# Softmax sums of unit 14 inverted over DRAM instead of on TensorE, and w4 tile 14 in two parts around the scores of unit 15

## The chip, the cores and the metric

The kernel runs on one core of a Trainium2 chip (trn2). The metric is the device time of one execution in microseconds; the median of three runs of the kernel before is 199.16 us (199.09 to 200.41). One further execution was profiled.

The engines are named as the profile names them: PE (TensorE, matmuls) and PEld (its weight loads), DVE (VectorE), ACT (ScalarE), POOL (GpSimd) and SP (SyncE, which here only issues DMAs). Each engine carries out its instructions in the order of the program; between engines there are semaphores. A DMA can be issued from SP, ACT or POOL.

## What is computed

A sequence of 2048 rows of 512 (bf16) is normalised and goes through two branches, A (attention) and B (two small MLPs), which are multiplied in a gate:

```python
xn = _layernorm(x)
# A: 32 heads of 16, each query sees 8 keys, at distances 0, 2, ..., 14 before it
q, k, v = split(xn @ wqkv)
attn = _softmax(where(mask, (q . kg) * scale, -1e9))   # kg, vg: gathered keys, values
s = concat_heads(attn . vg) @ wo
# B
h  = _gelu(_layernorm(xn) @ w1)
hs = shifted_quarters(h) @ w2
x1 = xn + hs
h2 = _gelu(_layernorm(x1) @ w3) @ w4
g  = _silu(x1 + h2)
return x + s * g
```

## The kernel before, in words

**Tiling.** The rows are kept as even rows (p = 0) and odd rows (p = 1), 1024 each, since the attention's distances are all even. A row tile is 128 rows; tile t = 8p + i, with i from 0 to 7. The first part (up to about 104 us) computes q, k and branch B up to the GELU of w3 (h3). The rest is a loop over **17 attention units** n = 0 to 16. Unit 0 holds the first rows of both halves, and units 1 to 8 (p = 0) and 9 to 16 (p = 1) hold 120 queries each.

**One iteration n**, in the order in which each engine gets its instructions:

- `scores(n)`, 32 small PE matmuls (L603) into PSUM `s` (4 banks); `weighted(n - 1)`, 64 PE matmuls (L650) of the previous unit's probabilities by its values into PSUM `o`. The lhs holds, beside each head's 16 values, 16 columns of the constant 2, so the softmax sums come out as rows of the same product. DVE adds the 8 columns where two key blocks meet (`mix`, L666, L667), and the function that `weighted` returns, called as `evict()`, copies the rest to SBUF on ACT (L668). Both write the tile `orw`.
- `exps(n)`, ACT (L614) from `s` to `prob`; `within(n)`, DVE (L623), cuts `prob` to the window.
- `values(n + 1)`, 4 PE matmuls (L582) into bank `b`, copied by ACT (L587).
- `w4_part(n, lo, hi)`, up to 11 PE matmuls (L529) of w4 for row tile n into bank `w`; with the last of them DVE adds the tile of x1 (L537), and the tile is put on a list of gates. `CUT` is 6. Tile 15 adds x1 on PE with an identity (L535).
- `gate_tanh` (ACT, L555) and `gate_mult` (DVE, L561) make the gate by a tanh for tiles up to 13; `gate_silu` (ACT, L547) by SiLU, whose table is loaded at L922, for tiles 14 and 15.
- from n = 6, `final(p, i)`: 4 PE matmuls (L802) by wo into bank `b`; its gate multiplies on DVE (L813, or L811 where the gate was made by SiLU with a factor 2) and adds x on POOL (L818); `store` writes two tiles (L844).

There is one bank `w`, one bank `b`, and one pair `o`. A matmul that starts a new use of a bank waits until the reader of the old use is done.

**Sums.** Units are joined in 11 runs. Runs 1 to 6 have two units each (run 6 is units 11 and 12), runs 7, 8, 9, 10 are units 13, 14, 15, 16. `moves` (L693) copies the 8 blocks of heads of `orw` to `oT`, one DMA each, on SP and POOL. The product in `oT` still has to be multiplied by the inverse of its softmax sum, and there are two ways for it:

- over DRAM, runs 0 to 7: `sums_gather` (two DMAs, L679, to `dn`), `sums_invert` (DVE reciprocal L757, then a DMA to DRAM, L759), `sums_read` (a DMA, L765, that spreads each inverse over 16 partitions and overwrites `orw`, so it also waits for the run's moves), `sums_apply` (L773, on DVE, for run 7 on POOL);
- on TensorE, runs 8, 9, 10: `sums_turn` (8 matmuls, L703), `sums_inverse` (DVE reciprocal L711 and two ACT copies L716), `sums_back` (4 matmuls, L741), `sums_mult` (DVE, L750, from PSUM). Runs 9 and 10 also go to `oT` by `rows` (8 matmuls L728, ACT copy L733) instead of moves.

**Which end which.** `final(1, i)` reads columns 128 i to 128 i + 127 of `oT`. With p = 1, run 7 is columns 544 to 663, run 8 664 to 783, run 9 784 to 903, run 10 904 to 1023. So final(1,4) needs run 7, final(1,5) runs 7 and 8, final(1,6) runs 8 and 9, final(1,7) runs 9 and 10.

**The order** is the one written in the program: at its end every instruction is made to follow the one before it on its engine. What is issued on one queue is therefore held up by a wait of anything ahead of it there. `R` is 11, `NN` is 17, `NC` is 3.

Of the kernel before, what the change touches and what calls it, by code (L numbers as in the profile page):

```python
# [15 lines left out]
def kernel(  # L16
# [22 lines left out]
    NF = (F + P - 1) // P  # L39
# [19 lines left out]
    NC = 3  # L59
# [462 lines left out]
    def w4_part(t, lo, hi, tag="w"):  # L522
        c, jj = t // TPC, t % TPC
        if lo == 0:
            banks["w4", t] = pst(tag, "w4_ps")[:, 0, :]
        pt = banks["w4", t]
        for ft in range(lo, hi):
            fs = P if ft < NF - 1 else FL
            pe.matmul(  # L529
                pt, lhsT=h3[c][:fs, ft, jj * P : (jj + 1) * P], rhs=w4_sb[:fs, ft, :],  # L530
                start=(ft == 0), stop=(ft == NF - 1 and t < NN - 2),
            )
        x_i = x_tile(c, jj)
        if hi == NF and t == NN - 2:
            pe.matmul(pt, lhsT=ident[:], rhs=x_i, start=False, stop=True)  # L535
        elif hi == NF:
            dve.tensor_tensor(out=x_i, in0=pt, in1=x_i, op=ALU.add)  # L537
            gates.append(t)
# [11 lines left out]
    def gate_tanh():  # L550
        for t in gates:
            if ("sig", t) in banks:
                continue
            sig = fin.tile([P, D], BF16, name="sig", tag="f")
            act.activation(sig, x_tile(t // TPC, t % TPC), AF.Tanh, scale=0.5)  # L555
            banks["sig", t] = sig
# [11 lines left out]
    def values(n):  # L568
        p, u = order[n]
        va = v_aug[n % NV]  # L570
        vp = pst("b", "v_ps")[:, 0, :]
        for dt in range(ND):
            first, last = dt == 0, dt == ND - 1
            if p is None:
                for s in range(2):
                    pe.matmul(
                        vp[KB * s : KB * s + KB, :], lhsT=xnT[s][:, dt, 0:KB], rhs=wv_sb[:, dt, :],
                        start=first, stop=last, tile_position=(0, KB * s),
                    )
            else:  # L580
                k0 = units[u]
                pe.matmul(vp, lhsT=xnT[p][:, dt, k0 : k0 + P], rhs=wv_sb[:, dt, :], start=first, stop=last)  # L582
        vs = vp.rearrange("p (h d) -> p h d", d=DH)
        if n == 0:
            dve.tensor_copy(out=va[:, :, 0:DH], in_=vs)  # L585
        else:
            act.activation(va[:, :, 0:DH], vs, AF.Copy)  # L587
        vas[n] = va
# [82 lines left out]
    rden = {}  # L671
    R = len(runs)

    def sums_gather(i):

        _, a, b, _, rw, parts = run_of(runs[i][0])
        dn = small.tile([P, H * rw // P], BF16, name="dn", tag="dn")
        for j in range(2):
            sp.dma_start(  # L679
                out=dn[P // 2 * j : P // 2 * (j + 1), :], in_=orw[i][DH : P : 32, ND * j : ND * (j + 1), :]  # L680
            )
        rden[i] = dn

    def moves(i, queues, part=None, heads=range(8)):

        _, a, b, _, rw, parts = run_of(runs[i][0])
        w = orw[i]
        for p, q0, c, nq in parts if part is None else [parts[part]]:
            if p not in oT:
                oT[p] = (midt if p == 0 else bigt)([P, ND, M], f"oT{p}")  # L690
            for hh in heads:
                jj, cg = divmod(hh, 4)
                queues[hh % len(queues)].dma_start(  # L693
                    out=oT[p][DH * hh : DH * (hh + 1), :, q0 : q0 + nq],
                    in_=w[32 * cg : 32 * cg + DH, ND * jj : ND * jj + ND, c : c + nq],
                )

    def sums_turn(i, tag):

        w = orw[i]  # L700
        pt = pst(tag, "dt_ps")[:, 0, 0:H].rearrange("p (g c) -> p g c", c=4)
        for g in range(2 * ND):
            pe.matmul(pt[0:QU, g, :], lhsT=w[:, g, :], rhs=ident[:, DH::32], start=True, stop=True)  # L703
        rden[i] = pt

    def sums_inverse(i, copy=lambda: None, behind=False):

        pt = rden[i]
        rb = small.tile([P, 2 * ND, 4], BF16, name="rbt", tag="rbt")
        with nc.allow_low_precision("bf16 weights"):  # L710
            dve.reciprocal(out=rb[0:QU], in_=pt[0:QU])  # L711
        if not behind:
            copy()
        rx = slot().rearrange("p (s j c d) -> p s j c d", s=ND, j=2, c=4)
        for j in range(2):
            act.activation(  # L716
                rx[0:QU, :, j], rb[0:QU, j * ND : (j + 1) * ND, :].unsqueeze(3).to_broadcast([QU, ND, 4, DH]), AF.Copy
            )
        if behind:
            copy()  # L720
        rden[i] = rx
# [46 lines left out]
    def sums_apply(i, eng=dve):  # L768
        _, a, b, _, rw, parts = run_of(runs[i][0])
        rr = rden.pop(i).rearrange("p (s q) -> p s q", s=ND)  # L770
        for p, q0, c, nq in parts:
            o = oT[p][:, :, q0 : q0 + nq]
            eng.tensor_tensor(out=o, in0=o, in1=rr[:, :, c : c + nq], op=ALU.mult)  # L773
# [69 lines left out]
    def store(q, p, i, n=2, cs=slice(0, D)):  # L843
        q.dma_start(  # L844
            out=ov[p, i * P : (i + n) * P, cs].rearrange("(i q) d -> q i d", q=P),
            in_=xo[p, i & ~1][:, i % 2 : i % 2 + n, cs],
        )
# [4 lines left out]
        load_xo(0, i)  # L852
    act.preload_act_table_set("exp_and_others")
    values(0)
    for n in range(NN - 1):
        scores(n)
        back = [i for i, (a, b) in enumerate(runs) if b == n - 2 and i < R - NC]
        done = [i for i, (a, b) in enumerate(runs) if b == n - 1]
        evict = weighted(n - 1) if n > 0 else lambda: None
        for i in back:  # L860
            sums_invert(i)
        exps(n, 2 if n == 0 else 1)
        if n == NN - 2:
            values(n + 1)
        evict()
        if 0 < n < NN - 2:
            values(n + 1)
        gate_mult()
        if n < NN - 2:
            gate_tanh()  # L870
        for i in done:
            if i < R - NC:
                sums_gather(i)
        if n == 2:
            moves(0, [sp, pool], 1)
        for i in back:
            if 0 < i < R - NC - 1:
                moves(i, [sp], None, [6, 7])
            sums_read(i)
        for i in done:  # L880
            if i == 0:
                moves(i, [sp, pool], 0)
            elif i < R - NC - 1:
                moves(i, [pool, sp], None, range(6))
            elif i == R - NC - 1:
                moves(i, [pool], None, range(4))
            else:
                moves(i, [pool, sp])
        if n == NN - 2:
            store(sp, 0, 6)  # L890
        within(n, 2 if n == 0 else 1)
        late = [i for i, (a, b) in enumerate(runs) if n == max(b + 3, 5)]
        w4_part(n, 0, NF if n < NN - 2 else CUT)
        if n == 0:
            values(n + 1)
        gate = final(*final_at[n]) if n in final_at else None
        if n == NN - 2:
            banks["end"] = True
            sums_turn(R - 3, "o")
            sums_inverse(R - 3)  # L900
            for i in late:
                sums_apply(i)
        if gate:
            gate(pool)
        if n < NN - 2:
            for i in late:
                sums_apply(i)
        if n == NN - 3:
            moves(R - NC - 1, [pool], None, range(4, 8))
        if n % 2 == 0 and 10 <= n < NN - 3:  # L910
            load_xo((n - 2) // 8, (n - 2) % 8)
        if n - 1 in final_at and n % 2 == 0 and n < NN - 3:
            p, i = final_at[n - 1]
            store(sp, p, i - 1)
        if n in (10, 12):
            load_xo(1, n - 6)
    scores(NN - 1)
    evict = weighted(NN - 2)
    store(sp, 1, 0)
    exps(NN - 1)  # L920
    evict()
    act.preload_act_table_set("silu_and_others")  # L922
    w4_part(NN - 2, CUT, NF)
# [1 line left out]
    within(NN - 1)  # L925
    gate2 = final(1, 2, "b")
    layout("high", f=1, g=1, h=1, i=1)
    sums_back(R - 3, "f")
    gate3 = final(1, 3, "h")
    sums_apply(R - 4, pool)  # L930
    evict = weighted(NN - 1, first=lambda: gate2(pool))
    evict()
    sums_turn(R - 2, "g")
    sums_inverse(R - 2, rows(R - 2, "i"), True)
    gate3(pool)
    store(sp, 1, 2)
    gate4 = final(1, 4, "w")
    sums_mult(R - 3)
    sums_turn(R - 1, "g")
    sums_back(R - 2, "f")  # L940
    sums_inverse(R - 1, rows(R - 1, "h"), True)
    sums_mult(R - 2)
    gate_silu(NN - 3)
    gate5 = final(1, 5, "b")
    gate4(pool)
    gate5(pool)
    store(sp, 1, 4)
    sums_back(R - 1, "i")
    gate6 = final(1, 6, "g")
    sums_mult(R - 1)  # L950
    halves = [slice(0, D // 2), slice(D // 2, D)]
    add6 = pe_add(1, 6, "o", slice(0, D))
    gate6(None)
# [48 lines left out]
```

## Time and profile before

| quantity | value |
|---|---|
| median of three runs | 199.16 us |
| profiled execution | 199.36 us |
| its span, first to last instruction | 197.6 us |
| granted TensorE clock | 1.00 |
| PE busy | 190.2 us (96%), 2591 matmuls |
| DVE busy | 125.1 us (63%) |
| ACT busy | 126.7 us (64%) |
| POOL busy | 61.8 us (31%) |

The span is counted from the first instruction; all times below are on that scale. Units 13 to 16 take up its end: `scores(14)` starts at 171.75, `scores(15)` at 177.05, `scores(16)` at 181.54, and the last store is issued at 194.4. A line of the profile in order of time has start, length, engine, line of the program, operation, output <- input, shapes, count, and in brackets the time that the engine was idle before, with what ended it. "SPq" is a DMA issue: its length is that of the issue, not of the transfer. Times of matmuls overlap a little, as they are pipelined. In the chain that ended last a piece begins where the one before it ends.

### The profile page before, as it was taken

The numbers are of one execution on the slowest core, as the hardware profiler recorded it, in microseconds if no ns is written. First come the engines' busy times: TensorE is split into PE (matmuls) and PEld (weight loads), VectorE is DVE, ScalarE is ACT, GpSimd is POOL, SyncE is SP. The second block draws the span as 40 slices with busy tenths as digits, with TensorE's granted clock in tenths as the row PEclk, the third lists the DMA queues.
The fourth block names the chain that finished last, engine by engine and source line by source line (L and its number), as shares of the span: only waits on it lengthen the run. The fifth ranks groups of instructions, "written<-read, shape, count | busy, mean of one in ns | idle before, by whom it ended". The sixth has DMA issues, their size and how long they took to land.

```text
span 197.6 us, 6164 instructions
## 1 busy us (share of the span) xinstructions
PE 190.2 (96%) x2591; PEld 98.5 (50%) x2591; DVE 125.1 (63%) x249; ACT 126.7 (64%) x140; POOL 61.8 (31%) x114
## 2 busy tenths in 40 slices
PE   7699999999999999999999999999999999999991
PEld 2588844444444444444444555555555554546550
DVE  4788856418539968200004776788888887786892
ACT  3559849644830643556558788887666676667961
POOL 4135722810200220200000533032626242469760
PEclk9999999999999999999999999999999999999999
DMA  5982181389452256460330012222232271713333
GB/s 158 304 281 84 60 268 53 122 151 339 140 154 62 76 137 167 121 140 0 119 117 3 12 22 66 73 49 69 44 101 62 59 207 31 233 33 88 88 119 108
DMA packets 33643, 22.32 MB, mean 113 GB/s; under 512 B 17584, under 2 KB 33104, under 8 KB 33616
## 3 DMA queue, kind: packets, MB, share of 16 engines
q1 hardware_dynamic: 32256, 21.06, 37.5%
q0 software_dynamic: 1216, 0.81, 2.1%
q8 instruction: 20, 0.33, 0.7%
q10 hardware_dynamic: 144, 0.07, 0.1%
q14 instruction: 7, 0.06, 0.1%
HBM read 12.41 MB, written 4.83 MB: 87 GB/s over the span
## 4 chain that ended last, share of the span: by engine, by line
PE 91%; DMA 3%; DVE 2%; SPq 1%; issue 1%; ACT 1%; DVEq 0%
PE w_ps L529 19%; PE w_ps L394 18%; PE qk_ps L297 13%; PE v_ps L582 8%; PE w_ps L354 7%; PE w_ps L330 7%; PE wo_ps L802 6%; PE o_ps L650 6%; DMA wqk_sb<-in_A_wqkv_dram 3%; PE s_ps L603 3%; PE w_ps L410 1%; PE tr_ps L265 1%; SPq L118 1%; PE dt_ps L703 1%; DVE oT L750 1%
## 5 line engine op out<-in xcount | busy, mean ns | idle before, releaser
L614 ACT ACTIVATE prob<-s_ps 128x2048 bf16<-128x2048 f32 (+1 forms) x18 | 31.9, 1781 | 18.0 <-PE s_ps L603 17.9
L529 PE MATMUL w_ps<-w_sb,h3T 128*128 128x512 bf16 (+1 forms) x176 | 40.8, 379 | 0.0
L398 ACT ACTIVATE h3T<-w_ps 128x1024 bf16<-128x1024 f32 x20 | 20.5, 1023 | 24.9 <-PE w_ps L394 24.9
L693 POOL DMA_DIRECT2D oT<-orw x38 | 19.4, 518 | 49.9 <-DVE orw L658 30.3
L394 PE MATMUL w_ps<-x1nT,w_sb 128*128 128x512 bf16 x160 | 35.0, 379 | 0.0
L297 PE MATMUL qk_ps<-xnT,wqk_sb 128*128 128x256 bf16 (+1 forms) x192 | 29.7, 308 | 1.2 <-DMA wqk_sb<-in_A_wqkv_dram 0.7
L529 PEld LDWEIGHTS <-h3T 128*128 128x128 bf16 (+1 forms) x176 | 17.1, 98 | 20.4
L394 PEld LDWEIGHTS <-w_sb 128*128 128x128 bf16 x160 | 15.6, 98 | 19.1 <-issue 0.4
L297 PEld LDWEIGHTS <-wqk_sb 128*128 128x128 bf16 x192 | 18.3, 98 | 11.2 <-DMA wqk_sb<-in_A_wqkv_dram 1.0
L623 DVE TENSOR_TENSOR prob<-prob,band 128x2048 bf16<-128x2048 bf16 (+1 forms) x18 | 21.0, 1167 | 2.9 <-ACT prob L614 2.7
L304 ACT ACTIVATE qT<-qk_ps,sel 128x1024 bf16<-128x1024 f32 x16 | 16.7, 1113 | 6.6 <-PE qk_ps L297 6.5
L818 POOL TENSOR_TENSOR xo<-sg,xo 128x512 bf16<-128x512 bf16 x9 | 11.7, 1304 | 21.5 <-DVE sg L813 21.5
L802 PE MATMUL wo_ps<-wo_sb,oT 128*128 128x512 bf16 (+1 forms) x68 | 16.6, 366 | 0.1
L582 PE MATMUL v_ps<-wv_sb,xnT 128*128 128x512 bf16 x64 | 16.6, 381 | 0.0
L359 DVE TENSOR_TENSOR xn<-w_ps,xn 128x1024 bf16<-128x1024 f32 x8 | 9.7, 1212 | 10.6 <-PE w_ps L354 10.6
L537 DVE TENSOR_TENSOR xn<-w_ps,xn 128x512 bf16<-128x512 f32 x15 | 10.4, 691 | 7.6 <-PE w_ps L529 7.5
L585 DVE CAST v_aug<-v_ps 128x512 bf16<-128x512 f32 x1 | 0.7, 691 | 22.5 <-ACT h3T L398 22.5
L668 ACT ACTIVATE orw<-o_ps 128x896 bf16<-128x896 f32 x16 | 14.6, 913 | 0.1
L330 PE MATMUL w_ps<-xn2T,w_sb 128*128 128x512 bf16 x64 | 14.5, 379 | 0.0
L354 PE MATMUL w_ps<-w_sb,hT 128*128 128x512 bf16 x64 | 14.3, 379 | 0.0
L650 PE MATMUL o_ps<-prob,v_aug 64*32 64x64 bf16 x1088 | 12.2, 195 | 0.1
L334 ACT ACTIVATE hT<-w_ps 128x1024 bf16<-128x1024 f32 x8 | 8.2, 1028 | 6.2 <-PE w_ps L330 6.2
(100 smaller groups left out, 236.0 us busy)
## 6 DMA issues: line engine op xcount, KB each, us to landing
x1n_dram<-xn SPq DMA_DIRECT2D x4, 512.0 KB
xn<-in_A_x_dram SPq DMA_DIRECT2D x6, 256.0 KB
xo<-in_A_x_dram SPq DMA_DIRECT2D x6, 256.0 KB
out_dram<-xo SPq DMA_DIRECT2D x6, 256.0 KB
orw<-rden_d SPq DMA_DIRECT2D x6, 240.0 KB
w_sb<-in_B_w_dram SPq DMA_DIRECT2D x1, 1376.0 KB
w_sb<-in_B_w_dram SPq DMA_DIRECT2D x1, 1280.0 KB
wqk_sb<-in_A_wqkv_dram SPq DMA_DIRECT2D x2, 512.0 KB
```

Source lines behind the costliest of these rows:

```text
L297: pe.matmul(pt[:, b, :], lhsT=wqk_sb[:, dt, nt * P : (nt + 1) * P], rhs=xnT[p][:, dt, ms], start=(dt == 0), stop=(dt == ND - 1),)
L330: pe.matmul(pt[:, b, :], lhsT=w1_sb[:, dt, g * P : (g + 1) * P], rhs=xn2T[:, dt, :], start=(dt == 0), stop=(dt == ND - 1),)
L354: pe.matmul(pt[:, j, :], lhsT=w2_src(p, g, m0), rhs=w2_sb[:, g, :], start=(g == 0), stop=(g == ND - 1),)
L394: pe.matmul(pt[:, b, :], lhsT=w3_sb[:, dt, ft * P : (ft + 1) * P], rhs=x1nT[:, dt, :], start=(dt == 0), stop=(dt == ND - 1),)
L398: act.activation(h3_tile(c)[:, 2 * a : 2 * a + 2, :], pt, AF.Gelu_apprx_tanh)
L529: pe.matmul(pt, lhsT=h3[c][:fs, ft, jj * P : (jj + 1) * P], rhs=w4_sb[:fs, ft, :], start=(ft == 0), stop=(ft == NF - 1 and t < NN - 2),)
L582: pe.matmul(vp, lhsT=xnT[p][:, dt, k0 : k0 + P], rhs=wv_sb[:, dt, :], start=first, stop=last)
L614: act.activation(pr[:, rs_], t[:, rs_], AF.Exp, scale=SCALE)
L623: dve.tensor_tensor(out=w, in0=w, in1=b.unsqueeze(1).to_broadcast([P, m, KB]), op=ALU.min)
L650: pe.matmul(op[32 * cg : 32 * cg + 32, s, g * KB : (g + 1) * KB], lhsT=va[KB * s : KB * s + KB, dt * 8 + h, :], rhs=pr[KB * s : KB * s + K ...
L693: queues[hh % len(queues)].dma_start(out=oT[p][DH * hh : DH * (hh + 1), :, q0 : q0 + nq], in_=w[32 * cg : 32 * cg + DH, ND * jj : ND * jj ...
L802: pe.matmul(pt, lhsT=oT[p][:, dt, i * P : (i + 1) * P], rhs=wo_sb[:, dt, cs], start=(dt == 0), stop=(dt == ND - 1),)
```

## The change

Run 8 (unit 14) takes the way over DRAM: its gather is issued half on SP and half on ACT, its moves one by one on SP and POOL between other steps, and its product is made by `sums_apply(8)` on DVE behind `sums_mult(9)`. `sums_turn(8)`, `sums_inverse(8)`, `sums_back(8)` and `sums_mult(8)` are gone. The last five matmuls of w4 tile 14 go from iteration 14 to iteration 15, behind `scores(15)` and `weighted(14)`. Iteration 15 is taken out of the loop and written by itself. In it `values(16)` comes behind `evict()` and the gather, so ACT's copy L587 follows L668; `gate_mult()` comes behind `within(15)`; `sums_apply(6)` moves from iteration 15 to behind `exps(16)`; the stores of (0,6) and (1,0) move later on SP; the gate of final(1,5) comes behind `sums_mult(10)`, and that of final(1,4) ahead of final(1,5) on the page.

The two parts of the loop that only lose their special cases for iteration 15 are left out:

```diff
-    def sums_gather(i):
+    def sums_gather(i, queues=(sp, sp)):
...
         for j in range(2):
-            sp.dma_start(
+            queues[j].dma_start(
...
-    for n in range(NN - 1):
+    for n in range(NN - 2):
...
-            elif i == R - NC - 1:
+            else:
                 moves(i, [pool], None, range(4))
-            else:
-                moves(i, [pool, sp])
-        if n == NN - 2:
-            store(sp, 0, 6)
         within(n, 2 if n == 0 else 1)
         late = [i for i, (a, b) in enumerate(runs) if n == max(b + 3, 5)]
-        w4_part(n, 0, NF if n < NN - 2 else CUT)
+        w4_part(n, 0, NF if n < NN - 3 else CUT)
...
-        if n == NN - 2:
-            banks["end"] = True
-            sums_turn(R - 3, "o")
-            sums_inverse(R - 3)
-            for i in late:
-                sums_apply(i)
         if gate:
             gate(pool)
...
+    n = NN - 2
+    scores(n)
+    evict = weighted(n - 1)
+    exps(n)
+    w4_part(n - 1, CUT, NF)
+    sums_invert(R - 4)
+    evict()
+    sums_gather(R - 3, (sp, act))
+    values(n + 1)
+    moves(R - 3, [sp, pool], None, range(4))
+    sums_read(R - 4)
+    moves(R - 3, [pool], None, range(4, 6))
+    within(n)
+    w4_part(n, 0, CUT)
+    gate_mult()
+    gate1 = final(1, 1)
+    banks["end"] = True
+    gate1(pool)
     scores(NN - 1)
     evict = weighted(NN - 2)
-    store(sp, 1, 0)
     exps(NN - 1)
+    sums_apply(R - 5)
+    moves(R - 3, [sp], None, range(6, 7))
+    sums_invert(R - 3)
+    moves(R - 3, [sp], None, range(7, 8))
+    store(sp, 0, 6)
+    sums_read(R - 3)
     evict()
...
     gate2 = final(1, 2, "b")
     layout("high", f=1, g=1, h=1, i=1)
-    sums_back(R - 3, "f")
     gate3 = final(1, 3, "h")
     sums_apply(R - 4, pool)
     evict = weighted(NN - 1, first=lambda: gate2(pool))
+    store(sp, 1, 0)
     evict()
...
     gate4 = final(1, 4, "w")
-    sums_mult(R - 3)
     sums_turn(R - 1, "g")
     sums_back(R - 2, "f")
     sums_inverse(R - 1, rows(R - 1, "h"), True)
     sums_mult(R - 2)
     gate_silu(NN - 3)
+    sums_apply(R - 3)
+    gate4(pool)
     gate5 = final(1, 5, "b")
-    gate4(pool)
+    sums_back(R - 1, "i")
+    sums_mult(R - 1)
     gate5(pool)
     store(sp, 1, 4)
-    sums_back(R - 1, "i")
     gate6 = final(1, 6, "g")
-    sums_mult(R - 1)
```

More of the change, by code (lines that the diff above doesn't have):

```diff
@@ L854 @@
     values(0)
-    for n in range(NN - 1):
+    for n in range(NN - 2):
         scores(n)
-        back = [i for i, (a, b) in enumerate(runs) if b == n - 2 and i < R - NC]
+        back = [i for i, (a, b) in enumerate(runs) if b == n - 2]
         done = [i for i, (a, b) in enumerate(runs) if b == n - 1]
@@ L862 @@
         exps(n, 2 if n == 0 else 1)
-        if n == NN - 2:
-            values(n + 1)
         evict()
-        if 0 < n < NN - 2:
+        if 0 < n:
             values(n + 1)
         gate_mult()
-        if n < NN - 2:
-            gate_tanh()
+        gate_tanh()
         for i in done:
-            if i < R - NC:
-                sums_gather(i)
+            sums_gather(i)
         if n == 2:
@@ L876 @@
         for i in back:
-            if 0 < i < R - NC - 1:
+            if i > 0:
                 moves(i, [sp], None, [6, 7])
@@ L896 @@
         gate = final(*final_at[n]) if n in final_at else None
-        if n == NN - 2:
-            banks["end"] = True
-            sums_turn(R - 3, "o")
-            sums_inverse(R - 3)
-            for i in late:
-                sums_apply(i)
         if gate:
             gate(pool)
-        if n < NN - 2:
-            for i in late:
-                sums_apply(i)
+        for i in late:
+            sums_apply(i)
         if n == NN - 3:
```

## The prediction, made before the changed kernel was run

> **What bounds the kernel now.** I read first the busy time by stage for the end of the kernel, because the change touches only what follows 173 us.
>
> ```profile
> 175.00:180.00 5.00, 5.00 (x116) 2.54 (x115) 4.32 (x9) 3.45 (x6) 4.02 (x7) 1.00 0.25 55
> 180.00:185.00 5.00, 4.91 (x123) 3.02 (x122) 3.25 (x7) 3.71 (x5) 4.28 (x8) 1.00 0.33 83
> 185.00:190.00 5.00, 5.00 (x115) 3.17 (x112) 4.40 (x10) 4.84 (x10) 3.51 (x3) 1.00 0.37 115
> 190.00:197.00 7.00, 3.38 (x23) 1.79 (x21) 3.64 (x8) 1.92 (x5) 2.27 (x2) 1.00 0.34 115
> ```
>
> Columns: stage, its length, then busy us of PE, PEld, DVE, ACT, POOL, the granted clock, DMA share, GB/s. PE is full until 190 us at clock 1.00 and no other engine is. After 190 us nobody is full, so there order and latency decide. The chain that ended last, second, shows the same hand-over.
>
> ```profile
> 180.35 0.86 PE wo_ps L802 x4
> 181.21 0.41 PE dt_ps L703 x8
> 181.62 0.02 issue
> 181.65 0.37 DVE rbt L711
> 182.02 0.04 issue
> 182.06 0.68 PE o_ps L650 x64
> ...
> 185.00 0.21 PE rr_ps L741 x4
> ...
> 189.41 0.66 DVE oT L750
> 190.07 0.81 DVE slots L813 x2
> 190.88 0.37 issue
> 191.25 0.66 DVE oT L750
> ```
>
> Columns: start, length, what. Unit 14's sums are on it: eight turn matmuls (0.41), a wait until DVE's reciprocal frees bank o (0.44, up to 182.06), four back matmuls (0.21). From 189 us DVE carries the chain. Third, the instructions in order of time, for two things the change will lean on: when bank b becomes free, and how long the sums take over DRAM.
>
> ```profile
> 173.71 2.54 PE L529 MATMUL w_ps<-w_sb,h3T 128*128 128x512 bf16 x11
> 174.91 0.60 ACT L587 ACTIVATE v_aug<-v_ps 128x512 bf16<-128x512 f32 x1
> 176.09 1.03 PE L802 MATMUL wo_ps<-wo_sb,oT 128*128 128x512 bf16 x4
> 179.08 0.63 SPq L759 DMA_DIRECT2D rden_d<-rb  x1
> 182.66 0.65 SPq L765 DMA_DIRECT2D orw<-rden_d  x1
> 185.64 1.25 POOL L773 TENSOR_TENSOR oT<-oT,orw 128x480 bf16<-128x480 bf16 x1 [0.78 <-DMA orw<-rden_d]
> ```
>
> final(1,0) (176.09) writes bank b, which the copy L587 reads until 175.51: today it has 0.58 us to spare. And run 7, of unit 13, needs 6.56 us from writing its inverses (179.08) to their use (185.64).
>
> **The change part by part.** The profiled execution took 199.36 us, span 197.6 and 1.76 around it; the median of three is 199.16. I work out a shift of the end in the profile and add it to the median.
>
> *Removed.* 0.41 + 0.44 + 0.21 = 1.06 us of PE's chain. ACT loses two L716 (182.04 to 182.67), which lie ahead of exp(16); DVE loses L711 (0.36) and exchanges L750 (0.65, from PSUM) for L773 at 480 wide. The trace has that at 256 (0.28) and 960 (0.65); between them, 0.40.
>
> *Tile 14 in two parts.* In the chain a whole tile of eleven matmuls takes 2.38 us (173.88), the six of tile 15 1.29 (179.06) and its five, apart, 1.19 (182.74): the split costs 0.10 by itself, and 2.38 - 1.29 = 1.09 leave the place before final(1,0). That would bring it from 176.09 to 175.00, but it must wait for bank b until 175.51 + 0.05 (the lag that 182.06 shows behind the reciprocal): another 0.56, so PE loses 0.66. ACT can't bring L587 forward, since exp(14) (172.34), L668 and L587 run back to back from scores that are not moved. Queued behind it is all of PE. So unit 15's scores come 0.53 earlier, at 176.52, not 1.09. weighted(14) at 176.88 is covered: its within ended at 176.32. If bank b cost nothing, all below would be 0.56 earlier. The addition L537 (0.69) moves ahead of recip(7) on DVE, hidden: w4 part two ends at 178.75, L537 at 179.5, recip(7) at 179.8, within(15) at 181.0, needed at 182.4.
>
> *Gather on ACT's queue.* exp(15) 177.05 to 178.93, L668 to 179.74, then the issue of half the gather. SP's gather halves take 0.58 each (1.18 to 1.23 a pair); ACT's one DMA row, a store, 0.37. A store of that size on SP takes 0.35 to 0.40 too, so the length goes by the transfer and I take 0.58. Queued behind it on ACT is the copy L587 of values(16): now 180.40 to 181.00, so final(1,1) starts at 181.05 where PE would be there at 180.85: 0.20 lost (0 at 0.37). It was copied ahead of L668 before, at 179.35; that order is given up.
>
> The Trainium skill (DMA: Bandwidth & Descriptors, Rules for kernel authors) says that spreading DMAs over engines saves only issue time, since all use the same 16 DMA engines, and advises against halving a transfer by partitions. By it the split could bring at most that one issue; here the ACT half leaves at 179.8 and the SP half, behind run 7's write, at 180.2, against 180.2 and 180.8 on SP alone, and the sum would be the same.
>
> *PE to the last unit.* final(1,1) ends at 182.08 (before: 181.22), scores(16) 182.44, exp(16) 182.54 to 184.42 (before 182.67 to 184.53). So the ACT time removed comes back as a late start. o_ps(15) to 183.05, w4 part two and the identity to 184.46, final(1,2) and (1,3) to 186.18 (before 186.08). The 1.06 removed is paid for by 0.66, 0.20 and the turn's cover: scores(16) ran inside the reciprocal's wait anyway. weighted(16) needs within(16); DVE brings gate 1, mix and add of unit 15, sums_apply(6) (183.7 to 184.35), recip(8) (184.3 to 184.63), within(16) to 185.85. Covered, if the gather has landed by 184.6. The last gather of run 6, issued at 170.3, let recip start at 174.12: 3.8 us, so 180.2 gives 184.0. Behind a late recip wait within(16), gate 2 and the last unit on PE: each 1 us over costs about 1 us.
>
> PE then runs as before, 0.1 late: turn(10) ends at 189.04 (188.94), recip(10) 189.43, sums_mult(9) 189.50 to 190.15 (189.41 to 190.07).
>
> *Round trip.* SP: write(8) at 184.66 (0.33), move 7 at 185.05 (0.65), the store of (0,6) 0.45, then the read. It overwrites orw, so it waits for write and moves. Rows for landing: POOL's moves 1.9 to 2.5 by size, extremes 1.7 and 3.8; run 2's write at 132.74 let its read start at 134.57 (under 1.9), run 7's at 179.08 only at 182.66. Middle of the moves, 2.2: read at 187.25 (186.75 to 188.85). Run 7's read took 2.98 to its use, same size: sums_apply(8) can start at 190.2, about when DVE comes free of sums_mult(9), 190.15.
>
> The Trainium skill (DMA: Bandwidth & Descriptors, Anatomy of one DMA) fits about 2.0 us a DMA plus size over 436 GB/s, measured on GpSimd's path and not on SP's. An estimate by it: 120 KB in 2.3 us, use at 189.6, so DVE would decide at 190.15 and the sum would be 0.05 less. Run 7's 2.98 is longer, and the row is used.
>
> *The end.* final(1,5) ran before from 189.56, sums_mult(8) having ended at 188.73. Now it waits: 190.2 + 0.40 + 0.05 = 190.65. It is followed by back(10) at +0.87, 0.38 long (190.44, 190.82 before), so sums_mult(10) starts at 192.0 against 191.25: +0.75. gate 5's L813 (0.67), done before sums_mult(10) until now, stands behind it and ahead of gate 6: +0.67, with nothing to hide it, since gate 6, pe_add, the last two matmuls and gate 7 follow one another to the last store. Sum +1.42: 200.78 against 199.36; on the median 200.6.
>
> **The rivals.**
> 1. *The round trip is late* (slower by over 1%). The place is SP's read of run 8. At the longest landing, 3.8, it leaves at 188.85 and sums_apply(8) starts at 191.85, 1.65 after the forecast's: 202.2. For it: run 7 took 3.58 from write to read; seven DMA issues of unit 14 share SP with it. Against: DMA share is 0.37 here, and runs 2 and 5 show 1.83 and 2.83. It decides from a read that leaves after 187.2, where DVE's own 190.15 is passed.
> 2. *PE's gain arrives* (not slower). The place is bank b. If neither final(1,0) nor final(1,1) waits there, all 1.06 of PE is kept: turn(10) ends at 188.94 - 1.06 = 187.88, sums_mult(9) at 189.0, and the trip, whose every step hangs on unit 14's and 15's order, moves up with it. sums_apply(8) at 189.0 instead of 190.2 gives 1.42 - 1.2 = +0.2: 199.4, inside the spread of the runs before (199.09 to 200.41) and not slower; what else I have priced too high takes it to 198.9. For it: the copy is only 0.6 long, and PE holds no other cause to wait. Against: 175.51 lies ahead of the change's first effect, so nothing moves it. It decides when final(1,0) starts before 175.2.
> 3. *The sums leave PE but nothing follows* (the change doesn't do what it says): DVE's recip(8) waits for a gather that lands at 184.6 or later, so within(16) waits as exp(16) did. At 185.0, +0.4 on the forecast: 201.0, inside its bounds.
>
> **How the numbers follow.** Forecast, third rival included, 0.55, with its own range 199.9 to 201.4; late trip 0.15; PE's gain 0.26; anything else 0.04, half on either side. The likeliest is 200.6. From 198.9 to 202.0 leaves out half of the late trip (0.08), a third of the second rival (0.08) and the rest (0.04). One per cent, 2 us, is about what a measurement of this kernel can tell from no change: the lines are 197.2 and 201.15. Slower: 0.15 + 0.07 of the forecast's upper end + 0.02 = 0.24. Faster: 0.03, since all that is removed is 1.06 of PE and some ACT time. Within: 0.73.
>
> **What would show it.** final(1,0) starting at 175.56 right behind L587; ACT's gather issue of some 0.58 ahead of L587 near 180.4; weighted(16) near 186.1; L773 on DVE near 190.2, with final(1,5) behind it and gate 5 behind sums_mult(10) near 192.0. I am wrong if final(1,0) doesn't wait, if DVE idles for dn ahead of within(16), or if L773 waits for the read by over 0.5 us.

## The result, and the profile after

The changed kernel takes 201.21 us (median of six, 200.89 to 202.08) where the kernel before takes 199.14 in the same comparison: ratio 1.0106, 95% interval 1.0080 to 1.0132, so about 2.07 us slower. Forecast were 200.6 and a range of 198.9 to 202.0. Of the prediction's two lines at one per cent the upper one, 201.15, falls inside the interval, so whether the change costs more or less than one per cent is not decided. The profiled execution took 200.91 us, span 199.2.

Two of the stages that the prediction showed, in the changed kernel (columns: stage, length, busy us of PE, PEld, DVE, ACT, POOL, granted clock, DMA share, GB/s):

```profile
180.00:185.00 5.00, 3.96 (x109) 1.94 (x109) 2.99 (x8) 3.14 (x3) 3.21 (x6) 1.00 0.34 76
185.00:190.00 5.00, 4.93 (x105) 2.90 (x105) 3.11 (x7) 3.97 (x7) 4.12 (x3) 1.00 0.43 130
```

PE is no longer full between 180 and 185 us: 3.96 us of 5 against 4.91. Turning to the instructions in order of time, the same profile shows what it waits for, and what stands in the end:

```profile
174.89 1.02 PE L802 MATMUL wo_ps<-wo_sb,oT 128*128 128x512 bf16 x4 [0.52 <-ACT v_aug L587]
179.19 1.09 ACTq L679 DMA_DIRECT2D dn<-orw  x1
180.32 0.60 ACT L587 ACTIVATE v_aug<-v_ps 128x512 bf16<-128x512 f32 x1 [1.17 <-issue]
180.97 1.02 PE L802 MATMUL wo_ps<-wo_sb,oT 128*128 128x512 bf16 x4 [0.60 <-ACT v_aug L587]
184.66 1.90 PE L802 MATMUL wo_ps<-wo_sb,oT 128*128 128x512 bf16 x8 [0.29 <-DVE oT L773]
187.08 0.65 SPq L765 DMA_DIRECT2D orw<-rden_d  x1
190.13 0.66 DVE L750 TENSOR_TENSOR oT<-rr_ps,oT 128x480 bf16<-128x480 f32 x1
190.70 0.40 DVE L773 TENSOR_TENSOR oT<-oT,orw 128x480 bf16<-128x480 bf16 x1
191.15 1.04 PE L802 MATMUL wo_ps<-wo_sb,oT 128*128 128x512 bf16 x4 [0.80 <-DVE oT L773]
192.51 0.66 DVE L750 TENSOR_TENSOR oT<-rr_ps,oT 128x480 bf16<-128x480 f32 x1 [0.81 <-PE rr_ps L741]
193.09 0.68 DVE L813 TENSOR_TENSOR slots<-wo_ps,xn 128x512 bf16<-128x512 f32 x1
193.68 1.01 DVE L811 SCALAR_TENSOR_TENSOR slots<-wo_ps,xn 128x512 bf16<-128x512 f32 x2
195.83 0.37 ACTq L844 DMA_DIRECT2D out_dram<-slots  x1
```

Three times a final product waits on PE ahead of `weighted(16)`: final(1,0) for bank b (0.52), final(1,1) for the same bank, whose copy L587 stands behind ACT's gather issue (0.60), and final(1,2) for sums_apply(6) (0.29). Then final(1,5) waits 0.80 for sums_apply(8), and the gate of final(1,5) (193.09) stands between sums_mult(10) (192.51) and the gate of final(1,6) (193.68).

**A common zero.** Two profiles can't be laid over each other by their own clocks. exp(14), which the change doesn't touch, starts at 172.34 in the profile of before and at 171.66 after. The difference is made near 9 us, where before the first products wait 0.74 us for the load of their weights, and after they don't wait for it. Before, with the last store:

```profile
9.29 1.05 PE L297 MATMUL qk_ps<-xnT,wqk_sb 128*128 128x256 bf16 x8 [0.74 <-DMA wqk_sb<-in_A_wqkv_dram]
172.34 1.88 ACT L614 ACTIVATE prob<-s_ps 128x2048 bf16<-128x2048 f32 x1 [1.68 <-PE s_ps L603]
194.04 0.37 ACTq L844 DMA_DIRECT2D out_dram<-slots  x1
```

and after:

```profile
6.73 2.85 PE L297 MATMUL qk_ps<-xnT,wqk_sb 128*128 128x256 bf16 x24 [0.40 <-DVE xnT L280]
171.66 1.88 ACT L614 ACTIVATE prob<-s_ps 128x2048 bf16<-128x2048 f32 x1 [1.50 <-PE s_ps L603]
```

So every profile below is measured from its own start of exp(14). Starts in us from there (the experiments are described below):

| kernel | final(1,1) | weighted(16) | sums_mult(9) | sums_apply(8) | final(1,5) | sums_mult(10) | last store on ACT |
|---|---|---|---|---|---|---|---|
| before | 7.85 | 13.67 | 17.07 | none | 17.23 | 18.91 | 21.70 |
| forecast, from before's 172.34 | 8.71 | 13.76 | 17.16 | 17.86 | 18.31 | 19.66 | 23.12 |
| after | 9.31 | 14.83 | 18.47 | 19.04 | 19.49 | 20.85 | 24.17 |
| e1_gather_sp | 8.61 | 14.26 | 17.69 | 18.69 | 19.16 | 20.75 | 25.07 |
| e3_apply6_early | 9.22 | 14.69 | 18.09 | 18.66 | 19.12 | 20.47 | 23.79 |
| e4_turn_on_pe | 8.67 | 14.89 | 18.60 | none | 18.75 | 20.11 | 23.43 |
| e5_apply8_first | 9.22 | 14.75 | 19.45 | 19.13 | 19.59 | 20.95 | 24.27 |
| e6_stores_later | 9.44 | 14.83 | 18.74 | 18.41 | 18.88 | 20.24 | 23.56 |
| e7_no_apply8 | 9.21 | 14.60 | 18.24 | none | 18.39 | 19.75 | 23.07 |
| e8_turn_later | 7.83 | 13.56 | 18.03 | none | 18.14 | 19.82 | 22.61 |
| c1_combined | 8.68 | 14.07 | 18.58 | 18.25 | 18.72 | 20.40 | 23.19 |
| b_again | 7.73 | 13.64 | 17.04 | none | 17.20 | 18.88 | 21.67 |
| a_again | 9.44 | 14.83 | 18.46 | 19.23 | 19.69 | 21.05 | 24.37 |

Counted so, the end comes 2.47 us later after the change than before; in the pair that was repeated, 2.70. The medians say 2.07 and 1.9, with intervals of 0.5 and 0.75 us either way, and in both profiles of after the beginning was 0.7 to 1.0 us shorter than in those of before.

### The profile page after: what moved, and what is told of

It is laid out like the page before. It is cut to its first block, busy times and chain, and to the rows that moved or that the text cites. A ratio compares the mean times of both kernels' runs of the same rounds, so it can differ in the third digit from the quotient of the medians.

```text
span 199.2 us, 6126 instructions
## 1 busy us (share of the span) xinstructions
PE 189.0 (95%) x2553; PEld 98.0 (49%) x2579; DVE 124.2 (62%) x249; ACT 126.2 (63%) x138; POOL 62.8 (32%) x114
## 4 chain that ended last, share of the span: by engine, by line
PE 74%; DMA 10%; DVE 5%; ACT 3%; POOL 3%; issue 2%; SPq 1%; ACTq 0%; DVEq 0%; POOLq 0%
PE w_ps L394 17%; PE qk_ps L297 14%; PE w_ps L529 12%; PE w_ps L354 7%; PE w_ps L330 7%; PE v_ps L582 6%; DMA oT<-orw 4%; PE o_ps L650 3%; PE wo_ps L802 2%; PE s_ps L603 2%; DMA dn<-orw 2%; ACT orw L668 2%; DMA out_dram<-xo 1%; PE w_ps L410 1%; DMA orw<-rden_d 1%
## 5 line engine op out<-in xcount | busy, mean ns | idle before, releaser
L529 PE MATMUL w_ps<-w_sb,h3T 128*128 128x512 bf16 (+1 forms) x173 | 40.3, 379 | 0.5 <-issue 0.3
L582 PE MATMUL v_ps<-wv_sb,xnT 128*128 128x512 bf16 x50 | 15.8, 382 | 0.7
L668 ACT ACTIVATE orw<-o_ps 128x896 bf16<-128x896 f32 x16 | 14.6, 912 | 1.0 <-PE row_ps L728 1.0
```

The source lines that it names most:

```text
L529: pe.matmul(pt, lhsT=h3[c][:fs, ft, jj * P : (jj + 1) * P], rhs=w4_sb[:fs, ft, :], start=(ft == 0), stop=(ft == NF - 1 and t < NN - 2),)
L668: return lambda: act.activation(wide(ow, c, KB, m), wide(ov_, 0, CH + W, m), AF.Copy)
```

## The experiments

Each ratio is to the kernel before, run on the same chip in between. Median times are beside it.

**The two kernels again, unchanged** (`b_again`, `a_again`).

> The kernel before the change once more, unchanged, as a measure of what two times and two profiles of one program differ by. In the profiles so far exp(14), ahead of everything the change touches, starts anywhere from 171.66 to 173.62 us, while what follows it repeats. Expected: ratio 1.000 within 0.003; from the start of exp(14) to the issue of the last store on ACT 21.7 us, as in the profile of before, within 0.2.

> The changed kernel once more, unchanged. Expected: ratio 1.0106 within 0.003; from the start of exp(14) to the issue of the last store on ACT 24.2 us within 0.3, of the issue of half a gather on ACT 1.09 us.

Before: 1.0013 (0.9985 to 1.0041), 199.61 us; after: 1.0094 (1.0057 to 1.0132), 201.12. The last two rows of the table repeat the first and third within 0.2 us, though the beginnings differ by 0.36 us between the two profiles of before. So what follows exp(14) repeated within 0.2 us in these two pairs, and less than that is read from no single row below; a difference of medians under 0.3% says little here.

**Part of the change undone: run 8's sums on TensorE again** (`e4_turn_on_pe`).

```diff
-    sums_gather(R - 3, (sp, act))
...
     banks["end"] = True
+    sums_turn(R - 3, "o")
+    sums_inverse(R - 3)
...
-    sums_invert(R - 3)
-    sums_read(R - 3)
...
+    sums_back(R - 3, "f")
     gate3 = final(1, 3, "h")
...
     gate4 = final(1, 4, "w")
+    sums_mult(R - 3)
...
-    sums_apply(R - 3)
```

> The changed kernel with its order, but run 8's sums are inverted on TensorE as before the change (turn behind final(1,1), back ahead of final(1,3), sums_mult behind sums_mult of nothing else, ahead of the turn of run 10); its gather, its trip to DRAM and sums_apply(8) are gone. Theory T: final(1,1) no longer waits behind the gather issue, final(1,5) no longer waits for sums_apply(8); what stays is the wait of final(1,0) and the split (0.6 us), the late sums_apply(6) and the later place of gate 5: about 199.9, range 199.6 to 200.3. Rival U (only the round trip costs): 199.2, as before the change.

1.0045 (1.0025 to 1.0065), 200.31 us. The way over DRAM is thus worth about 0.6% of the 1.06%, and the split with the new order about 0.45%. By the table, 0.74 of 2.47 us comes back. What stays: final(1,1) 0.82 late (bank b at final(1,0), the split), weighted(16) 1.22 late (final(1,2) still waits 0.21 for the late sums_apply(6)), and 0.53 at the end. That last is the gate of final(1,5): from sums_mult(10) to the last store it takes 2.79 us in the rows with the old place (before, e8, c1) and 3.32 in the rows with the new one (after, e3 to e7; e1, told below, is an exception). Theory T's 199.9 was too low by 0.4, its range just missed; rival U's 199.2 is out.

**The tile whole again** (`e2_w4_whole`).

```diff
-        w4_part(n, 0, NF if n < NN - 3 else CUT)
+        w4_part(n, 0, NF)
...
-    w4_part(n - 1, CUT, NF)
```

> The changed kernel, but all eleven matmuls of w4 tile 14 in iteration 14. Theory T: final(1,0) no longer waits for bank b (0.52 us in the changed kernel), but unit 15's scores and ACT's exp(15), L668, the 1.09 us of gather issue and the copy of values(16) come about 0.5 us later, while TensorE reaches final(1,1) earlier, so the wait there grows from 0.60 to about 1.9 us: 0.3 to 0.6 us slower than the changed kernel, 201.6. Rival V (the wait of final(1,0) is pure loss): 0.5 us faster, 200.7.

1.0173 (1.0135 to 1.0211), 202.70 us. Theory T's direction holds and rival V falls: given the gather on ACT, the split saves more than bank b takes. The size was larger than expected. In the profiled execution, at 204.25 us the slowest of six, the stages show a part of why (first the instruction in order of time, then stages of 1 us, the clock third from the right):

```profile
183.20 1.02 PE L802 MATMUL wo_ps<-wo_sb,oT 128*128 128x512 bf16 x4 [2.06 <-ACT v_aug L587]
```

```profile
183.00:184.00 1.00, 0.80 (x4) 0.29 (x3) 0.00 (x0) 0.15 (x1) 0.91 (x2) 1.00 0.33 64
184.00:185.00 1.00, 1.00 (x82) 0.68 (x80) 0.69 (x1) 0.26 (x1) 0.00 (x0) 0.68 0.33 72
185.00:186.00 1.00, 1.00 (x42) 0.51 (x30) 0.45 (x2) 1.00 (x1) 0.96 (x1) 0.50 0.38 110
```

After 2.06 us without a matmul TensorE is granted half its clock; the stage from 188 us is the first at 1.00 again. By the mean granted clock that didn't happen in every execution: it is 0.989 and 0.990 in the two slowest of the six, and 0.997 or more in the four others, which took 201.81 to 203.10 us (median 202.3). So the long wait alone seems to make this kernel slower than the changed one, and the clock adds to it in some executions. Also, the issue of half the gather on ACT took 1.42 us here.

**The gather on SP alone** (`e1_gather_sp`).

```diff
-    sums_gather(R - 3, (sp, act))
+    sums_gather(R - 3)
```

> The changed kernel, but both halves of run 8's gather are issued on SP. Theory T (TensorE's waits count): in the changed kernel the issue on ACT took 1.09 us ahead of the copy L587 of values(16), and final(1,1) waited 0.60 us for that copy. Without it L587 starts about 1.1 us earlier, final(1,1) doesn't wait for it, and the end comes 0.4 to 0.6 us earlier: 200.7 where the changed kernel took 201.2. Rival U (the round trip over DRAM sets the end whatever TensorE does): the second half of the gather leaves no earlier than before, so the end stays within 0.2 us of 201.2.

1.0100 (1.0067 to 1.0134), 201.19 us. Theory T is right as far as unit 16: no wait at final(1,1) any more, 0.70 us earlier there and 0.57 at weighted(16). But the time is rival U's. The read leaves SP 0.60 earlier and is used only 0.35 earlier: DVE is there first and waits 0.34, and PE waits 1.24 behind it (the profile puts the 0.34 down to the store under way; sums_apply(8) uses the read's tile):

```profile
187.16 0.65 SPq L765 DMA_DIRECT2D orw<-rden_d  x1
191.03 0.41 DVE L773 TENSOR_TENSOR oT<-oT,orw 128x480 bf16<-128x480 bf16 x1 [0.34 <-DMA out_dram<-xo]
191.50 1.08 PE L802 MATMUL wo_ps<-wo_sb,oT 128*128 128x512 bf16 x4 [1.24 <-DVE oT L773]
```

In the profiled execution (202.4 us, the slowest of six) that wait too was followed by half a clock: 0.68 in the stage from 192 us, 0.50 in the next two, 0.61 in that from 195, which is why its row ends at 25.07. The five others had a mean clock of 0.996 or more, so the row's last two columns are not those of the median. With the steps of the changed kernel behind final(1,5) (4.68 us) the row would end at 23.84, an estimate: 0.33 are left of the 0.70. Two of the stages:

```profile
191.00:192.00 1.00, 0.50 (x3) 0.27 (x4) 0.97 (x2) 0.66 (x2) 0.00 (x0) 1.00 0.68 242
192.00:193.00 1.00, 1.00 (x8) 0.69 (x7) 0.04 (x1) 0.00 (x0) 0.83 (x1) 0.68 0.00 0
```

**Both halves on ACT** (`g_act_both`, a single execution): `(act, act)` in the same place.

> The changed kernel with both halves of run 8's gather on ACT. It tells why the issue on ACT took 1.09 us where SP's take 0.58. Theory S (ACT's issue was stretched because SP issued at the same time: SP's write of run 7 and half of the gather fall into it): at least one of the two now takes about 0.6 us. Rival (an issue of this transfer takes 1.09 us on ACT): both take 1.09. In either case final(1,1) waits longer, by 0.5 to 1.1 us, and the end is later.

The two issues by themselves (shortest, median and longest in ns, then the starts of the first and the last in us):

```profile
L679 ACTq DMA_DIRECT2D dn<-orw x2: 534/814/1094, 180.0 to 181.1; - x2
```

The first took 1.09 us and the second 0.53, so 1.09 is not the length of this transfer's issue on ACT as such: theory S's condition is met and the rival is out. What stretches the first is not shown. SP issues a DMA during both of them, so the reason that theory S gives, an issue on SP at the same time, is not enough by itself. final(1,1) waits 1.15, and the run took 202.17 us.

**sums_apply(6) earlier** (`e3_apply6_early`).

```diff
+    sums_apply(R - 5)
     gate1(pool)
...
-    sums_apply(R - 5)
```

> The changed kernel, but sums_apply(6) stands on DVE ahead of the gate of final(1,1), where it stood before the change, instead of behind mix and addition of unit 15. final(1,2) reads the columns of run 6. Theory T: the wait of final(1,2) for L773 (0.29 us on TensorE, 0.78 on its weight loads) goes, and the end comes 0.2 to 0.3 us earlier: 200.9. Rival U: unchanged, 201.2.

1.0125 (1.0082 to 1.0168), 201.25 us: no gain in the time. The wait of final(1,2) is gone, but it has moved. sums_apply(6) now waits 1.80 us for the moves of its run, mix of unit 15 comes behind it, within(16) later, and weighted(16) waits for within(16):

```profile
186.66 0.68 PE L650 MATMUL o_ps<-prob,v_aug 64*32 64x64 bf16 x64 [0.35 <-DVE prob L623]
```

By the table weighted(16) gains 0.14, which is within the 0.2 of a repeat, and the end 0.38; the medians can't confirm it.

**When does the read land?** (`e5_apply8_first`, `e6_stores_later`). The second has the first's edit too.

```diff
+    sums_apply(R - 3)
     sums_mult(R - 2)
     gate_silu(NN - 3)
-    sums_apply(R - 3)
```

```diff
-    store(sp, 0, 6)
...
-    store(sp, 1, 0)
...
-    store(sp, 1, 2)
...
     sums_apply(R - 3)
+    store(sp, 1, 2)
+    store(sp, 0, 6)
+    store(sp, 1, 0)
     sums_mult(R - 2)
```

> The changed kernel, but sums_apply(8) stands on DVE ahead of sums_mult(9) instead of behind it. Where DVE then idles before it, the read of run 8 has not landed. Theory L (the read's landing decides): it lands some 3.6 us after its issue, so DVE idles 0.4 to 0.6 us before sums_apply(8), final(1,5) starts at most 0.2 us earlier, and the time is that of the changed kernel, 201.2, or up to 0.4 us more since sums_mult(9) is now behind the wait. Rival D (DVE's order decides; run 7's read took 2.98 us to its use): no idle time before it, final(1,5) starts 0.65 us earlier, 200.6.

> As the run with sums_apply(8) first, and the three stores of 256 KB each, (0,6), (1,0) and (1,2), stand on SP behind the read of run 8, in the order (1,2), (0,6), (1,0), so that none of them is issued before the third gate of the end is done. Theory C (the read is slow because the stores share the DMA engines with it): it lands 3.0 us after its issue instead of 3.6, final(1,5) starts 0.6 us earlier than with the stores ahead, and the time is 200.6. Rival (the read's length is its own): it lands as late as in the run before, and the time is 201.2 or more.

With sums_apply(8) first, DVE stands idle for the read (in order of time):

```profile
187.61 0.65 SPq L765 DMA_DIRECT2D orw<-rden_d  x1
188.31 2.64 SPq L844 DMA_DIRECT2D out_dram<-xo  x2
191.41 0.41 DVE L773 TENSOR_TENSOR oT<-oT,orw 128x480 bf16<-128x480 bf16 x1 [0.84 <-DMA orw<-rden_d]
```

and with the stores behind it no longer:

```profile
187.35 0.65 SPq L765 DMA_DIRECT2D orw<-rden_d  x1
...
190.54 1.45 SPq L844 DMA_DIRECT2D out_dram<-xo  x3
190.57 0.41 DVE L773 TENSOR_TENSOR oT<-oT,orw 128x480 bf16<-128x480 bf16 x1
```

From issue to use it is 3.80 us with a 256 KB store issued 0.70 us after it (and one 1.1 us before), at most 3.22 with none near. Theory L holds for that order: the read's landing sets sums_apply(8). In the changed kernel itself it is close to a tie: DVE doesn't idle before sums_apply(8), which comes 3.62 us after the read's issue, and in `a_again` it comes 3.82 after it, 0.11 behind sums_mult(9). Theory C holds in this pair, but the stores don't stretch the read by a fixed amount: in `e3_apply6_early`, with the same store 0.71 us behind it, the read was used without a wait 3.47 us after its issue. The records of single packets in the traces agree: from the first to the last of the read's 128 packets it is 1.60 us in e5, 0.97 in e6, and 0.98 in `e7_no_apply8`, where the store stands as in e5. The Trainium skill (DMA: Bandwidth & Descriptors, Issuing engines are not separate DMA queues) has all DMAs of a core on the same 16 engines, interleaved; the pair e5 and e6 agrees. Ratios: 1.0121 (1.0088 to 1.0154), 201.50 us, and 1.0098 (1.0065 to 1.0131), 201.09; the table has the second's end 0.71 us ahead of the first's, as theory C expected of final(1,5); the medians show 0.4 of it.

**Without the last step** (`e7_no_apply8`): sums_apply(8) left out.

> The changed kernel without sums_apply(8): run 8's columns stay without the product by the inverse of their sums; gather, reciprocal, write and read are all still issued. This prices what hangs on the end of the round trip. Theory L: final(1,5) starts behind rows(10), 0.8 us earlier, sums_mult(10) follows, and the end comes 0.8 to 1.1 us earlier: 200.2, about the run with TensorE's inversion (200.3). Rival (TensorE's waits before unit 16 are the whole price): 0.3 us earlier at most, 200.9.

1.0081 (1.0056 to 1.0105), 200.88 us; by the table, final(1,5) and the end are 1.10 us earlier than after the change. Of that, 0.23 is there already at weighted(16), ahead of the step left out, so 0.87 hangs on the step, as theory L has it. The median moved by 0.3 only and lies where the rival put it: the rival is out by the profile, not by the times.

**All of it together** (`c1_combined`): the edits of e1, e5 and e6, sums_apply(6) directly behind the gate of final(1,1), and the gate of final(1,5) ahead of sums_back(10).

> The changed kernel with all that the single runs point to: the gather on SP alone, sums_apply(6) between the gate of final(1,1) and mix of unit 15, the three stores behind the read of run 8 with (1,2) first, sums_apply(8) ahead of sums_mult(9), and the gate of final(1,5) ahead of sums_mult(10) as before the change. Theory: the terms add up: final(1,1) 0.6 us, final(1,2) 0.3 us and the read some 0.6 us earlier, the gate of final(1,5) 0.2; from exp(14) to the last store on ACT 22.6 us against 24.2 of the changed kernel and 21.7 of the kernel before, so 200.0, still slower than before. Rival (a further wait takes the place of those removed): 23.3 us or more, 200.7.

1.0037 (1.0011 to 1.0064), 200.31 us: better than the changed kernel, still behind the one before. The end is at 23.19, between the theory's 22.6 and the rival's 23.3. The terms didn't quite add up:

```profile
184.13 0.96 DVE L773 TENSOR_TENSOR oT<-oT,orw 128x960 bf16<-128x960 bf16 x1 [0.79 <-DMA rden_d<-rb]
...
188.10 0.66 SPq L765 DMA_DIRECT2D orw<-rden_d  x1
191.16 0.41 DVE L773 TENSOR_TENSOR oT<-oT,orw 128x480 bf16<-128x480 bf16 x1 [0.86 <-DMA orw<-rden_d]
```

Moved ahead, sums_apply(6) waits 0.79 for a DMA, and reciprocal, write and read of run 8 stand behind it. So the read leaves only 0.23 us earlier than in the changed kernel, not 0.6. It now takes 3.06, and DVE still waits 0.86 for it.

**The kernel before, with its own stall taken out** (`e8_turn_later`).

```diff
-            sums_turn(R - 3, "o")
-            sums_inverse(R - 3)
...
-    sums_back(R - 3, "f")
+    sums_turn(R - 3, "g")
+    sums_inverse(R - 3)
     gate3 = final(1, 3, "h")
...
     evict()
+    sums_back(R - 3, "f")
```

> The kernel before the change, but sums_turn(8) and sums_inverse(8) move from behind final(1,1), where they hold bank o for 0.44 us, to behind final(1,2) into bank g, and sums_back(8) behind unit 16's weighted matmuls. Theory T: scores(16) and exp(16) start 0.4 to 0.9 us earlier and unit 16's weighted matmuls some 0.4 us earlier; the time is 198.9 where the kernel before takes 199.3. Rival: the end's order on DVE takes it back, 199.3.

1.0093 (1.0058 to 1.0128), 201.05 us. The stall of 0.44 is gone, and weighted(16) gains 0.11; then ACT's two copies of the inverse stand behind the table load (185.84, 1.28 us) and the SiLU, and PE waits for them. From the waits of that kernel (waiting line, what it waited for, us in total, times, longest):

```profile
PE rr_ps L741 <- ACT slots L716: 0.9, 1, 0.9
```

The end is 0.91 later. In the profiled execution, 2 us slower than that of before, another 0.89 lies ahead of exp(14), where the first products waited 1.24 us for their weights; whether that belongs to the program or to chance four runs don't say.

## Why the prediction was right in direction and short in size

The forecast shift was 1.42 us; the profile has 2.47, the medians 2.07. That 201.21 lies within the forecast's own bounds of 199.9 to 201.4 is in part luck: 2.47 us on the median of 199.16 would be 201.6, and the beginnings happened to be shorter after. "Slower" by over one per cent had a chance of 0.24 only, and the ratio, 1.0106, is a little above that line. Step by step, from exp(14):

- *Bank b at final(1,0)*: forecast start 3.22, measured 174.89 - 171.66 = 3.23. Right, and so was the 0.53 us that unit 15's scores gain.
- *Gather on ACT's queue*: the place was right (L587, and PE behind it), the size was not. "I take 0.58" was 1.09, in both profiles: a length taken over from SP's queue. final(1,1) waited 0.60 instead of 0.20 and starts at 9.31, not 8.71. This is the term that was mis-sized. A smaller part is the split of tile 14: with no gather on ACT final(1,1) starts at 8.61 to 8.68 (e1, e4, c1), where the prediction had PE ready at 8.51.
- *"sums_apply(6) (183.7 to 184.35)"*: its length was right (0.66 us), its start 0.92 late from exp(14), since PE was late. final(1,2) reads run 6's columns, and this reader was not named. Its wait of 0.29 us on PE was missing. Together with the term above it makes most of the 1.07 by which weighted(16) came later than forecast (14.83 against 13.76). Another 0.2 follows up to the turn of run 10: DVE's addition L667 of unit 16, which ACT's L668 needs, comes 0.27 behind mix, where before it followed at once; why stays open.
- *Gather in time*: right. DVE did not idle for dn ahead of recip(8) or within(16).
- *Round trip*: sums_apply(8) was forecast as a tie between the read and DVE, and nearly a tie it was, at 19.04 instead of 17.86. Both sides were late: DVE by 1.31, since PE was; the read because it left SP 0.51 late and took longer than the 2.98 of run 7 (it was used 3.62 us after its issue here, 3.82 in the repeat). So taking time out of PE and DVE alone gained less than it took out: in e1 sums_mult(9) came 0.78 earlier and sums_apply(8) 0.35.
- *Gate 5's place*: forecast 0.67, measured 3.32 - 2.79 = 0.53.

Sum against the forecast: sums_mult(10) 1.19 later, the gate's place 0.14 cheaper, 1.05 us in all.

Of the rivals, the late round trip was there in half: the read took longer, but it left SP late because its write (13.22, forecast 12.32) hangs on DVE's late steps. "PE's gain arrives" is refuted by final(1,0), which waited as forecast. The third, a recip(8) that waits for its gather, did not occur.

## What to carry to other kernels

When a step is moved on an engine, list every reader of its output, not only the instructions queued behind it: 0.29 us came from a reader on another engine. Where two paths meet late at the same point, undoing one shows little; price the point itself by taking out the step that joins them, and compare profiles from a common instruction ahead of the change. A length read on one engine's queue need not hold on another's: half the gather took 0.60 us to issue on SP and 1.09 on ACT. And the time from a DMA's issue to its use is a range: 3.06 to 3.87 us for one read, where DVE waited for it (c1, e1).

## What the runs showed of the hardware that was not expected

- A pause of TensorE can cost more than its length. In two profiles, after 2.06 us without a matmul (e2) and after 1.24 us (e1), the granted clock fell to 0.50; the four stages from 0.68 to 0.61 or 0.62 make about 3.4 us of half clock, an estimate from them. After 0.80 us (the changed kernel), 1.01 (`a_again`) and 1.15 (`g_act_both`) it stayed at 1.00. It is not the same in every execution: a mean clock of 0.988 to 0.990 stands in two of six executions of e2 and in one of six of e1, and 0.996 or more in the others. The Trainium skill (TensorE: Matmul & The Clock Gate, HAM oscillation) warns of gaps over about 3.4 us; in these two profiles shorter ones were enough.
- Issuing half the gather on ACT took 1.09 us in both profiles of the changed kernel and 1.42 in e2, on SP 0.60 for the other half; the second of two on ACT took 0.53 (`g_act_both`). The cause stays open.
- The load of the first weights held the first matmuls near 9 us for 0 (the changed kernel) to 1.92 us (`e7_no_apply8`), so times of one program differ by more than some of the effects studied here: the two profiles of before waited 0.74 and 0.99.
